# A gated recurrence and a bilinear feed-forward in one kernel: a new order of the first half, other engines for some of its work, and one transpose by DMA

## The chip, the cores and the metric

The kernel runs on one core of a Trainium2 chip. The core has TensorE (PE in the profile, PEld for its weight loads), VectorE (DVE), ScalarE (ACT), GpSimd (POOL) and SyncE (SP), which here only issues DMAs. The metric is the device time of one run in microseconds.

## The reference

Four sequences of 5824 tokens with 256 channels pass through a gated linear recurrence, and its output through a feed-forward without a nonlinearity:

```
log_a = 8 * sigmoid(r_gate) * log(clip(sigmoid(a_param)))
a     = exp(log_a);  norm = sqrt(max(1 - a*a, 1e-6))
h_t   = a_t * h_(t-1) + norm_t * sigmoid(i_gate_t) * x_t      # for every channel, along time
out   = (((h @ w1) * (h @ w2)) @ w3) @ w_out                  # 256 -> 1024 -> 1024 -> 256
```

## The kernel before

The 23296 tokens are cut into 47 chunks: two of 256 tokens that share tiles, 44 of 512, and one of 256. Time must lie along the free axis for the recurrence, so gates are turned from token rows to channel rows. For chunk c and channel half cb the steps are, with the one-letter names that the order uses:

- `r`, `i`, `x` load the three inputs; `R`, `I` are tanh on ScalarE (the sigmoid by way of tanh); `p` adds 1 to the input gate and `t` multiplies it by x, each half a chunk (`u_t`), on GpSimd or, if listed, on VectorE.
- `V` and `U` turn the decay gate and `u_t`. Chunks in `TURN_R` or `TURN_U` are turned by TensorE into PSUM (tile `ptr`), the others by a DMA transpose on SyncE into SBUF (tiles `rt` and `ut`).
- `d` is exp on ScalarE (`a_t`), `s` its square (`nrm`, on GpSimd, VectorE or ScalarE), `q` the root on ScalarE. tanh and exp share a table of ScalarE, the root has another: each change is an ACT_TABLE_LOAD.
- `g` multiplies the root by the turned `u_t` on VectorE, `h` is the scan on VectorE, `y` the cast of its result to bf16.
- `a` and `b` are the products with w1 and w2 (`pa`, `pb`), 128 features each for `a`, 256 for `b`; `c` copies `pa` to SBUF (`sa`, on ScalarE or, if in `DV_COPY`, on VectorE); `m` multiplies it by `pb` on VectorE (`g_t`).
- `D` multiplies `g_t` by the folded matrix w3 @ w_out (`po`), `e` copies the result out of PSUM, `o` stores it. The folding (`Ft`, `Fc`, `Fm`, `Fe`, tiles `ptw`, `w3t`, `pw`) is done in the kernel, between the first chunks, from eight pieces of w3 that are loaded (`L`) and cast (`C`). `W` is a pair of matmuls on the identity that has no use but to keep TensorE going while the first inputs arrive.

Nothing schedules this at build time. A string of 2449 words, ORDER, gives the order in which the steps are issued; since every engine works its own instructions in order, it fixes the order on each engine, DMA issues on SyncE included. Sets of indices (`DV_COPY`, `AC_SQUARE` and others) say which engine does a step. Buffers are rings: four PSUM slots (`po` in RINGS) are shared by `ptr`, `pa`, `ptw`, `pw` and `po`, two hold `pb`, and three each hold `sa` and `g_t`. A step that needs a slot waits until the last reader of its old content is done. The lines that matter here: `times` L175, `turn_pe` L194, `turn_dma` L207, `square` L225, `gated` L240, `scan` L254, `cast` L272, `copy` L325, `product` L332, `evac` L375, `fold_c` L432.

Of the kernel before, what the change touches and what calls it, by code (L numbers as in the profile page):

```python
# [664 lines left out]
```

## Time and profile before

| | |
|---|---|
| runs of the kernel before | 511.16, 511.36, 511.41 us (median 511.36) |
| span of the profiled execution, first to last instruction | 509.1 us |
| busy: TensorE, VectorE, ScalarE, GpSimd | 501.7, 431.8, 461.5, 318.0 us |
| ACT_TABLE_LOADs | 34 |

The span of the profiled execution is what the trace covers; its own launch time is not listed, and the runs are 2.3 us longer than its span. The busy time of TensorE is that of pipelined matmuls whose ends are modelled, so it is high even where matmuls start late. Times in the rows count from the start of the span.

### The profile page before, as it was taken

The page shows a single profiled execution, that of the slowest core. Times are in us where ns is not written, and L with a number is a line of the kernel's source. Part 1 is how long each engine was busy: PE and PEld are TensorE (multiplying, and loading weights), DVE is VectorE, ACT ScalarE, POOL GpSimd, SP SyncE. Part 2 cuts the span into 40 slices and gives each one's busy share as a digit, 9 for nine tenths or more (in the row PEclk, how much of TensorE's full clock was granted, in tenths as well). Part 3 has the DMA queues.
Part 4 walks back from the last instruction along what each step waited for, and adds up shares of the span by engine and source line. Part 5 has one row for each costly group of instructions (what it writes and reads, how often), then busy time and mean ns, then how long its engine had stood idle before and what let it go on. Part 6 is the DMA issues. An engine that isn't in the chain of part 4 may idle for free.

```text
span 509.1 us, 8891 instructions
## 1 busy us (share of the span) xinstructions
PE 501.7 (99%) x3225; PEld 308.3 (61%) x3225; DVE 431.8 (85%) x417; ACT 461.5 (91%) x708; POOL 318.0 (62%) x269
## 2 busy tenths in 40 slices
PE   7999999999999999999999999999999999999997
PEld 3767665665665656556656556565566655656566
DVE  6999999999999789879979799878877797959762
ACT  7999999998999999999999999998998979888543
POOL 1686677658658937964886973956647568580200
PEclk9999999999999999999999999999999999999999
DMA  8999999999989998896999997899886895252213
GB/s 317 410 411 345 335 316 282 305 286 259 310 220 298 279 285 247 211 302 196 247 305 327 254 286 148 252 243 227 210 246 164 235 298 161 85 166 62 65 51 104
DMA packets 178048, 124.06 MB, mean 244 GB/s; under 512 B 87378, under 2 KB 174036, under 8 KB 178004
## 3 DMA queue, kind: packets, MB, share of 16 engines
q1 hardware_dynamic: 178000, 123.50, 85.4%
q8 instruction: 25, 0.41, 0.4%
...
q10 hardware_dynamic: 4, 0.00, 0.0%
...
## 4 chain that ended last, share of the span: by engine, by line
PE 92%; ACT 3%; DMA 2%; POOL 1%; DVE 1%; issue 1%; SPq 1%; ACTq 0%; DVEq 0%
PE po L357 30%; PE pb L299 29%; PE pa L299 29%; DMA wf<-in_moe_w_dram 2%; PE pw L436 1%; ACT sa L322 1%; PE ptr L200 1%; PE ptw L425 1%; POOL u_t L192 0%; DVE h_t L270 0%; SPq L151 0%; ACT ot L322 0%; SPq L407 0%; ACT L168 0%; ACT L238 0%
## 5 line engine op out<-in xcount | busy, mean ns | idle before, releaser
L337 DVE TENSOR_TENSOR g_t<-sa,pb 128x1024 bf16<-128x1024 bf16 (+1 forms) x188 | 218.7, 1180 | 58.9 <-PE pb L299 27.6
L299 PEld LDWEIGHTS <-w_sb 128*128 128x128 bf16 x1504 | 146.4, 98 | 144.1 <-issue 1.4
L322 ACT CAST sa<-pa 128x512 bf16<-128x512 f32 (+1 forms) x332 | 179.8, 591 | 27.1 <-PE pa L299 18.9
L299 PE MATMUL pa<-y_t,w_sb 128*128 128x512 bf16 (+1 forms) x752 | 190.2, 372 | 0.2 <-ACT sa L322 0.2
L299 PE MATMUL pb<-y_t,w_sb 128*128 128x512 bf16 (+1 forms) x752 | 184.9, 372 | 0.2 <-ACT w_sb L414 0.2
L357 PE MATMUL po<-wp_sb,g_t 128*128 128x256 bf16 (+1 forms) x1464 | 177.6, 272 | 0.0
L357 PEld LDWEIGHTS <-g_t 128*128 128x128 bf16 x1464 | 142.5, 98 | 39.5 <-issue 0.3
L282 POOL CAST y_t<-h_t 128x1024 bf16<-128x1024 f32 (+2 forms) x47 | 53.8, 1145 | 140.2 <-DVE h_t L270 136.1
L192 POOL TENSOR_TENSOR u_t<-i_t,x_t 128x512 bf16<-128x512 f32 (+1 forms) x90 | 123.3, 1387 | 3.8 <-DMA ut<-u_t 1.8
L270 DVE TENSOR_TENSOR_SCAN h_t<-a_t,h_t,nrm 128x512 f32<-128x512 f32 (+1 forms) x92 | 121.1, 1343 | 1.6
L233 POOL TENSOR_TENSOR nrm<-a_t 128x512 f32<-128x512 f32 x70 | 78.4, 1137 | 7.0 <-ACT a_t L223 4.0
L223 ACT ACTIVATE a_t<-rt,la 128x512 f32<-128x512 bf16 (+1 forms) x82 | 66.1, 823 | 0.0
L322 ACT COPY ot<-po 128x512 f32<-128x512 f32 x84 | 49.1, 589 | 13.2 <-PE po L357 12.9
L173 POOL TENSOR_SCALAR i_t<-i_t 128x1024 f32<-128x1024 f32 (+1 forms) x45 | 55.4, 1233 | 8.3 <-ACT i_t L168 8.3
L251 DVE SCALAR_TENSOR_TENSOR nrm<-nrm,ut 128x1024 f32<-128x1024 f32 (+1 forms) x39 | 53.2, 1365 | 5.2 <-ACT nrm L238 5.2
L168 ACT ACTIVATE i_t<-i_t 128x1024 f32<-128x1024 f32 (+1 forms) x46 | 48.5, 1063 | 0.3 <-DMA i_t<-in_i_gate_dram 0.2
L238 ACT ACTIVATE nrm<-nrm 128x1024 f32<-128x1024 f32 (+1 forms) x47 | 48.4, 1040 | 0.2
L162 ACT ACTIVATE th_r<-r_t 128x1024 bf16<-128x1024 f32 (+1 forms) x41 | 43.5, 1064 | 0.0
L320 DVE CAST sa<-pa 128x512 bf16<-128x512 f32 x36 | 23.5, 684 | 1.4 <-PE pa L299 0.8
L238 ACT ACT_TABLE_LOAD x17 | 21.8, 1283 | 0.4
L287 PE MATMUL warm<-ident 128*128 128x512 bf16 x32 | 10.7, 473 | 1.6 <-DVE ident L441 1.6
L231 ACT ACTIVATE nrm<-a_t 128x512 f32<-128x512 f32 x18 | 11.4, 645 | 0.0
...
## 6 DMA issues: line engine op xcount, KB each, us to landing
r_t<-in_r_gate_dram SPq DMA_DIRECT2D x45, 512.0 KB, 5.2
i_t<-in_i_gate_dram SPq DMA_DIRECT2D x45, 512.0 KB, 6.0
x_t<-in_x_dram SPq DMA_DIRECT2D x45, 512.0 KB, 5.5
...
wf<-in_moe_w_dram SPq DMA_DIRECT2D x12, 512.0 KB, 10.5
wf<-in_moe_w_out_dram SPq DMA_DIRECT2D x2, 512.0 KB, 10.2
rt<-th_r SPq DMA_TRANSPOSE x41, 4.7
ut<-u_t SPq DMA_TRANSPOSE x39, 4.4
```

Of the source, the lines that this page charges most:

```text
L173: (nc.vector if c in DV_PLUS else nc.gpsimd).tensor_scalar(t, t, 1.0, 1.0, op0=ALU.add, op1=ALU.mult)
L192: (nc.vector if (c, half) in DV_HALF else nc.gpsimd).tensor_mul(out=u, in0=t, in1=xt)
L223: nc.scalar.activation(out=a, in_=pr, func=AF.Exp, scale=la4[:, cb:cb + 1], bias=la4[:, cb:cb + 1])
L233: (nc.vector if (c, cb) in DV_SQUARE else nc.gpsimd).tensor_mul(out=n, in0=a, in1=a)
L238: nc.scalar.activation(out=n, in_=n, func=AF.Sqrt, scale=-1.0, bias=1.0)
L251: nc.vector.scalar_tensor_tensor(out=n, in0=n, scalar=1e-3, in1=T["pu", c][:, :, cols], op0=ALU.max, op1=ALU.mult)
L270: nc.vector.tensor_tensor_scan(h[:, cb, :], a[:, cb, :], n[:, cb, :], init, ALU.mult, ALU.add)
L282: (nc.vector if key in DV_CAST else nc.gpsimd).tensor_copy(out=y, in_=h)
L299: nc.tensor.matmul(out=dst, lhsT=w_sb[:, cb, m * P:(m + 1) * P], rhs=T["y", gates_of(c)][:, cb, span(c, mp)], start=(cb == 0), stop=(cb == ...
L322: nc.scalar.copy(out=dst, in_=src_ps)
L337: nc.vector.tensor_mul(out=T["g", z][:, 2 * mp:2 * mp + 2, span(c, mp)], in0=T["sa", c, mp][:, :, :w], in1=T["pb", c, mp][:, :, :w])
L357: nc.tensor.matmul(out=po, lhsT=T["g", c][:, k, j * P:(j + 1) * P], rhs=wp_sb[:, k, cols], start=(k == 0), stop=(k == KD - 1), skip_group_ ...
```

## The change

Three things change. Chunk 6 leaves `TURN_U`: its `u_t` is turned by a DMA transpose. The sets that choose engines are new: `DV_COPY` grows from 36 to 62 entries and reaches to chunk 24, nine products `t` (`DV_HALF`) and a few other steps move to VectorE, `AC_SQUARE` grows from 18 to 23. And the first 1400 of the 2449 words of ORDER are in another order; from D23.2 on (the product of chunk 23's third block of 128 tokens) the words are the same. The number of table loads stays at 34.

```diff
-    TURN_U = {0, 2, 3, 4, 5, 6, 7}
+    TURN_U = {0, 2, 3, 4, 5, 7}
-    DV_HALF = set()
-    DV_SQUARE = {(0, 0), (0, 1), (5, 1), (9, 0)}
+    DV_HALF = {(2, 0), (12, 0), (15, 0), (18, 1), (19, 0), (21, 1), (23, 0), (25, 1), (26, 1)}
+    DV_SQUARE = {(0, 0), (0, 1), (26, 0)}
...
-    DV_CAST = {(1, 1)}
-    AC_CAST = {(1, 0)}
+    DV_CAST = {17, (1, 0)}
+    AC_CAST = {(0, 0), (0, 1)}
...
-    DV_EVAC = {(0, 0), (0, 1), (4, 1), (5, 1), (6, 1), (9, 0), (9, 1)}
-    FOLD_ACT = {('e', 0), ('e', 4), ('e', 5), ('e', 7)}
+    DV_EVAC = {(0, 1), (4, 0), (4, 1), (6, 1), (7, 0), (8, 1), (16, 0), (16, 1), (22, 1)}
+    FOLD_ACT = {('c', 3), ('c', 4), ('e', 1), ('e', 2), ('e', 3), ('e', 6)}
...
-    W_ACT = {('w2', 0), ('w3', 3)}
-    W_DVE = {('w1', 1)}
+    W_ACT = {('w3', 0)}
+    W_DVE = set()
...
-        r0 i0 x0 Lw1.1 Lw1.0 r2 i2 Lw2.0 Lw3.2 x2 E W13 A3. A0. A1. A2. R0.1 R0.0 W3 W10 V0.0 V0.1 I0 t0.1 d0.0 s0.0
+        E W9 W3 r0 A3. i0 A0. A1. W5 W7 W1 R0.0 V0.0 R0.1 V0.1 x0 Lw1.0 A2. I0 t0.0 W8 W6 t0.1 U0 d0.0 s0.0 W4
...
```

On ScalarE in the head, before (`nrm` is the root of chunk 0, `th_r` and `i_t` are chunk 2's gates, `y_t` is chunk 1's):

```order
L238 ACT_TABLE_LOAD
L238 ACTIVATE nrm<-nrm 128x2x256 x2
L160 ACT_TABLE_LOAD
L160 ACTIVATE th_r<-r_t 128x1024
L168 ACTIVATE i_t<-i_t 128x1024
L414 CAST w_sb<-wf 128x2x512
L280 CAST y_t<-h_t 128x256
L223 ACTIVATE a_t<-ptr,la_85 128x512 x2
```

and now (`y_t` is chunk 0's, both channel halves):

```order
L241 ACT_TABLE_LOAD
L241 ACTIVATE nrm<-nrm 128x2x256 x2
L163 ACT_TABLE_LOAD
L163 ACTIVATE th_r<-r_t 128x1024
L283 CAST y_t<-h_t 128x256 x2
L226 ACTIVATE a_t<-ptr,la_85 128x512 x2
L234 ACTIVATE nrm<-a_t 128x512
L171 ACTIVATE i_t<-i_t 128x1024
```

The cast of w2 and the tanh of chunk 2's input gate left this place; the two casts to chunk 0's `y_t` stand behind the table load and the tanh of `th_r`.

On VectorE at chunk 18, from the first scan of chunk 20 to the second (`g_t` is the product for chunk 18 or 19), before:

```order
L270 SCALAR_TENSOR_TENSOR h_t_2866<-a_t_2353,h_t_2790,nrm_2417 128x512
L337 TENSOR_TENSOR g_t_2899<-sa_2870,pb_2860 128x1024
L337 TENSOR_TENSOR g_t_2899<-sa_2826,pb_2909 128x1024
L337 TENSOR_TENSOR g_t_2899<-sa_2904,pb_2920 128x1024
L270 SCALAR_TENSOR_TENSOR h_t_2866<-a_t_2353,h_t_2790,nrm_2417 128x512
```

and now (`u_t` is chunk 21's):

```order
L273 SCALAR_TENSOR_TENSOR h_t_2858<-a_t_2296,h_t_2726,nrm_2463 128x512
L340 TENSOR_TENSOR g_t_2833<-sa_2781,pb_2862 128x1024
L340 TENSOR_TENSOR g_t_2833<-sa_2800,pb_2869 128x1024
L195 TENSOR_TENSOR u_t_2787<-i_t_2456,x_t_2713 128x2x2x128
L323 COPY ot_2909<-po_2892 128x512
L323 COPY ot_2930<-po_2913 128x512
L340 TENSOR_TENSOR g_t_2955<-sa_2843,pb_2940 128x1024
L340 TENSOR_TENSOR g_t_2955<-sa_2888,pb_2946 128x1024
L323 CAST sa_2975<-pa_2962 128x512
L273 SCALAR_TENSOR_TENSOR h_t_2858<-a_t_2296,h_t_2726,nrm_2463 128x512
```

Three products stood between the two scans; now four stand there, with one product `u_t`, two copies of `po` and one of `pa`.

On SyncE, where the decay gate of chunk 9 is turned (the first transpose into `rt`; the second is chunk 8's), before:

```order
L380 DMA out_dram<-ot 128x2x256
L151 DMA i_t<-in_i_gate_dram 128x4x256
L151 DMA r_t<-in_r_gate_dram 128x4x256
L211 DMA_TRANSPOSE rt<-th_r 128x8x128
L380 DMA out_dram<-ot 128x2x256
L151 DMA r_t<-in_r_gate_dram 128x4x256 x2
L211 DMA_TRANSPOSE rt<-th_r 128x8x128
```

and now (the transpose into `ut` is chunk 6's):

```order
L383 DMA out_dram<-ot 128x2x256
L154 DMA r_t<-in_r_gate_dram 128x4x256
L154 DMA x_t<-in_x_dram 128x1024
L214 DMA_TRANSPOSE ut<-u_t 128x8x128
L214 DMA_TRANSPOSE rt<-th_r 128x8x128
L383 DMA out_dram<-ot 128x2x256
L154 DMA i_t<-in_i_gate_dram 128x4x256
L383 DMA out_dram<-ot 128x2x256
L154 DMA i_t<-in_i_gate_dram 128x4x256
L214 DMA_TRANSPOSE rt<-th_r 128x8x128
```

The transpose into `ut` is new and stands ahead of the two others; TensorE's eight transposes of chunk 6 are gone.

## Rows read from the trace of the kernel before

**Rows 1.** Chain of waits by engine and line, 26.38 to 276.25 us (shares).
```profile
by line: PE pb L299 32.0%; PE pa L299 31.8%; PE po L357 31.5%; PE pw L436 2.4%; PE ptw L425 1.3%; PE ptr L200 1.1%
```

**Rows 2.** Pieces of that chain, 30 to 60 us: start, us, what.
```profile
35.25 0.45 PE ptr L200 x8
...
48.77 1.75 PE po L357 x16
...
50.52 1.73 PE pb L299 x8
```

**Rows 3.** TensorE by line and shape, 26.38 to 276.25: xcount | busy, mean ns | idle.
```profile
L299 PE MATMUL pa<-y_t,w_sb 128*128 128x512 bf16 x368 | 96.1, 379 | 0.0
...
L357 PE MATMUL po<-wp_sb,g_t 128*128 128x256 bf16 x720 | 88.4, 273 | 0.0
```

**Rows 4.** Busy us (instructions) of each engine by stretch, clock, DMA share, GB/s.
```profile
0.00:26.40 26.40, 22.32 (x162) 13.85 (x163) 20.64 (x45) 23.08 (x30) 11.41 (x18) 1.00 0.95 366
26.40:150.00 123.60, 123.60 (x841) 77.66 (x840) 121.38 (x134) 120.47 (x173) 85.06 (x70) 1.00 1.06 308
150.00:276.30 126.30, 126.30 (x779) 75.97 (x778) 108.36 (x89) 123.58 (x192) 90.48 (x72) 1.00 0.96 265
276.30:509.10 232.80, 229.49 (x1449) 140.80 (x1447) 181.41 (x152) 194.39 (x316) 131.07 (x111) 1.00 0.69 184
```

**Rows 5.** Pieces of the chain of waits, 0 to 26.38 us.
```profile
4.66 10.66 DMA wf<-in_moe_w_dram
...
17.52 2.51 POOL u_t L192 x2
...
20.07 0.51 PE ptr L200 x6
```

**Rows 6.** Timeline of the head: start, us, engine, line, operation, [idle before it].
```profile
7.08 0.69 DVE L189 SCALAR_TENSOR_TENSOR u_t<-i_t,x_t 128x512 bf16<-128x512 f32 x1 [1.62 <-DMA x_t<-in_x_dram]
...
9.31 1.15 ACT L238 ACTIVATE nrm<-nrm 128x512 f32<-128x512 f32 x2
...
10.36 0.75 DVE L248 SCALAR_TENSOR_TENSOR nrm<-nrm,ptr 128x256 f32<-128x256 f32 x2 [0.18 <-PE ptr L200]
...
10.48 1.28 ACT L160 ACT_TABLE_LOAD   x1
...
11.77 1.06 ACT L160 ACTIVATE th_r<-r_t 128x1024 bf16<-128x1024 f32 x1
...
13.11 1.04 PE L299 MATMUL pa<-y_t,w_sb 128*128 128x256 bf16 x8
...
22.73 2.49 DVE L270 TENSOR_TENSOR_SCAN h_t<-a_t,h_t,nrm 128x512 f32<-128x512 f32 x2
...
25.28 1.04 POOL L282 CAST y_t<-h_t 128x1024 bf16<-128x1024 f32 x1 [2.32 <-DVE h_t L270]
...
26.38 0.81 PE L299 MATMUL pa<-y_t,w_sb 128*128 128x512 bf16 x3
```

**Rows 7.** DMA transposes into ut, whole span: issue to landing.
```profile
DMA to landing us min/median/max: 2.7/4.4/6.9
```

**Rows 8.** Copies of pa on ScalarE and VectorE, whole span.
```profile
L322 ACT CAST sa<-pa 128x512 bf16<-128x512 f32 x324 | 177.1, 596 | 21.9 <-PE pa L299 14.9 <-DVE g_t L337 6.0
...
L320 DVE CAST sa<-pa 128x512 bf16<-128x512 f32 x36 | 23.5, 684 | 1.4 <-PE pa L299 0.8
```

**Rows 9.** VectorE's scans and gated products, 150 to 276.25 us: busy, mean ns | idle.
```profile
L270 DVE TENSOR_TENSOR_SCAN h_t<-a_t,h_t,nrm 128x512 f32<-128x512 f32 x25 | 35.4, 1434 | 0.5
...
L251 DVE SCALAR_TENSOR_TENSOR nrm<-nrm,ut 128x1024 f32<-128x1024 f32 x13 | 17.7, 1364 | 1.2 <-ACT nrm L238 1.2
```

**Rows 10.** Durations of scans and gated products, whole span: ns min/median/max, first to last start.
```profile
L270 DVE TENSOR_TENSOR_SCAN h_t<-a_t,h_t,nrm x92: 727/1279/2379, 13.2 to 487.8; 128x512 f32<-128x512 f32 x88, 128x256 f32<-128x256 f32 x4
...
L251 DVE SCALAR_TENSOR_TENSOR nrm<-nrm,ut x39: 686/1222/2105, 89.5 to 485.4; 128x1024 f32<-128x1024 f32 x38, 128x512 f32<-128x512 f32 x1
...
L251 DVE SCALAR_TENSOR_TENSOR nrm<-nrm,ptr x2: 1212/1216/1221, 61.0 to 65.9; 128x1024 f32<-128x1024 f32 x2
```

More of the change, by code (lines that the diff above doesn't have):

```diff
@@ new lines @@
+        c9.3.0 e8.1 i16 h11.0 o7.1 a10.3.0 c10.3.0 D8.1 D8.0 I16 a9.3.1 V16 a10.1.1 r17 e8.0 t12.0 a10.3.1
+        c9.3.1 V14 h11.1 y11 b9.3 m9.3 b10.3 a10.2.0 d16.0 U13 c10.1.1 c10.3.1 m10.3 a10.2.1 c10.2.1 x15 R17
+        a10.1.0 c10.1.0 b10.2 c10.2.0 d14.1 m10.2 p15 b10.1 d16.1 m10.1 s13.0 d14.0 p14 a11.0.0 s15.1 a11.0.1
+        c11.0.1 o8.1 c11.0.0 q12 a11.2.0 c11.2.0 b11.0 U12 t15.1 m11.0 a11.1.1 a11.3.1 c11.3.1 s16.0 o7.0
+        c11.1.1 g12 s14.0 D10.3 D10.2 e10.1 i17 t15.0 h12.0 a11.1.0 c11.1.0 h12.1 o8.0 D10.1 s16.1 a11.2.1
@@ new lines @@
+        d23.0 I24 s23.1 a18.2.0 V24 c18.2.0 D15.0 D15.1 e15.0 d24.1 o14.1 U20 r26 b18.0 m18.0 d24.0 a18.1.1
+        c18.1.1 a19.1.0 c19.1.0 I22 i25 o15.1 r27 a18.2.1 p22 t22.1 g20 h20.0 x23 b18.1 m18.1 c18.2.1 b18.2
+        m18.2 I23 V25 o15.0 t21.1 a19.0.1 x24 a19.0.0 c19.0.0 c19.0.1 I25 D16.2 D16.3 e16.1 U21 D16.1 D16.0
+        e16.0 o16.0 a19.3.0 a19.1.1 o16.1 b19.1 p25 b19.0 t22.0 c19.3.0 c19.1.1 m19.1 U22 R26 m19.0 a19.2.1
+        D17.3 p24 c19.2.1 d25.0 r32 h20.1 d25.1 s22.1 R27 a18.3.1 c18.3.1 D17.2 e17.1 a18.3.0 s21.0 c18.3.0
@@ new lines @@
+        R28 s25.1 c21.1.1 R30 c21.0.1 g23 b21.0 d27.0 a21.2.1 o18.0 D19.0 m21.0 D19.1 c21.2.1 e19.0 o19.0 I26
+        a21.1.0 c21.1.0 p26 h23.0 d27.1 s27.1 i27 a21.3.1 c21.3.1 a21.3.0 c21.3.0 x28 b21.1 a21.2.0 m21.1
+        c21.2.0 b21.3 m21.3 a22.1.0 c22.1.0 a22.1.1 c22.1.1 d26.1 s26.1 D19.3 b21.2 m21.2 R32 V28 a22.0.0
+        c22.0.0 t25.1 V30 t26.1 a22.2.0 c22.2.0 D19.2 e19.1 x27 a22.0.1 o19.1 I27 c22.0.1 b22.1 m22.1 b22.0
+        a22.2.1 c22.2.1 t25.0 h23.1 y23 D20.3 U25 a22.3.1 d28.1 s28.1 c22.3.1 D20.2 x29 e20.1 m22.0 b22.2
@@ new lines @@
+        m29.0 a29.2.1 e27.0 d33.1 a29.2.0 c28.3.0 c29.2.0 c29.2.1 x33 a28.3.1 c28.3.1 r38 g32 b29.1 m29.1 I36
+        b29.2 t31.1 t34.0 a30.0.0 m29.2 D27.2 c30.0.0 R35 s34.1 I35 o25.1 a30.0.1 b28.3 U31 d36.0 D27.3 e27.1
+        o27.0 m28.3 a29.3.0 s33.0 s33.1 p33 t34.1 b30.0 c30.0.1 c29.3.0 a30.2.0 a29.3.1 c29.3.1 i37 b29.3
+        a30.3.0 c30.2.0 d36.1 g31 m30.0 a30.1.0 V35 m29.3 b30.1 D28.0 D28.1 c30.3.0 o27.1 U34 x35 V37 a30.1.1
+        i38 q34 h31.0 h31.1 a30.2.1 h32.0 h32.1 b30.2 c30.1.0 e28.0 D28.2 D29.0 c30.1.1 t33.0 t33.1 o28.0
@@ new lines @@
+        m42.0 q43 g43 h43.0 h43.1 c42.1.0 c42.2.0 e41.0 U45 a42.1.1 a42.2.1 c42.1.1 q45 a42.3.0 c42.3.0 q44
+        D40.2 D40.3 e40.1 c42.2.1 b42.2 a42.3.1 o40.0 y43 c42.3.1 m42.1 x46 g45 m42.2 b43.0 U44 g44 o40.1
+        a43.0.1 a43.0.0 a43.1.0 c43.0.0 c43.0.1 b42.3 a43.1.1 a43.2.0 m42.3 m43.0 h44.0 h44.1 c43.1.0 c43.1.1
+        a43.3.0 c43.2.0 D41.2 D41.3 a43.2.1 b43.1 y44 c43.3.0 e41.1 m43.1 c43.2.1 o41.0 o41.1 a43.3.1 b43.2
+        D42.0 D42.1 e42.0 c43.3.1 o42.0 m43.2 h45.0 h45.1 b44.0 a44.0.0 a44.0.1 a44.1.1 a44.1.0 c44.0.0 y45
@@ L631 @@
+        b46.0 D44.2 D44.3 e44.0 b46.1 c46.0.1 c46.2.1 a46.1.1 D45.0 D45.1 c46.1.1 m46.0 e44.1 m46.1 b46.2
+        a46.3.1 a46.3.0 b46.3 D45.2 D45.3 e45.0 c46.3.0 c46.3.1 o44.0 o45.0 e45.1 o44.1 o45.1 m46.2 m46.3 D46.0
+        D46.1 e46.0 e46.1 o46.0 o46.1
         """
```

255 lines of the change are left out of this document (118 added, 137 removed), and 9 rows, old and new, of the table DV_COPY.

## The prediction

> **What bounds the kernel now.** I read the chain of waits first, then counts and busy time by stretch, and last the head instruction by instruction. From 26.38 us, where chunk 2's first product starts, to 276.25, where the new order falls back into the old one, every piece of the chain is TensorE's: the six shares of [rows 1] add up to 100.1%. A TensorE that is always on the chain may still stand still between matmuls, whose ends are modelled, so the reader should check by count. Matmuls follow each other at 1.73 / 8 = 0.216 us (512 columns) and 1.75 / 16 = 0.109 us (256 columns) [rows 2]. The stretch holds 368 of pa and as many of pb, 736 x 0.216 = 159.0; 720 of po, 720 x 0.109 = 78.5; and the 4.8% of the folding and the transposes, 12.0 [rows 1, 3]. That is 249.5 of 249.9 us: about 0.4 us is lost. ScalarE and VectorE only have to keep up there, and they do, at 97% and 98% up to 150 us, and at 98% and 86% from 150 to 276 [rows 4].
>
> What is not matmul work lies ahead of 26.38. There the chain runs over weight loads that land at 15.32, then over GpSimd to the two products for chunk 2's gated input, and to the transposes at 20.07 that wait for them [rows 5]. Beside it a chain on VectorE leads from chunk 0's input at 7.08 over the first gated product at 10.36 and chunk 2's scans, done at 25.22, to chunk 2's y at 26.32 [rows 6]. So there are three places: the head, 26 to 276 us, and the rest.
>
> **The change part by part.** The profiled span is 509.1 us and the median of the runs 511.36; the 2.3 us between them lie around the span, and I carry them over.
>
> *Chunk 6's gated input by DMA.* TensorE loses 8 transposes, 0.45 us [rows 2], all on the path: -0.45. SyncE gains one transpose, which lands 4.4 us after its issue at the median and 6.9 at worst [rows 7]. Its cover: it is issued once chunk 6's two products are there, and after them GpSimd still makes chunk 5's two (2.51 for two, [rows 5]), and VectorE a gated product (1.36, [rows 9]) and two scans (2.49, [rows 6]), before chunk 6's gated product is due: 6.4 us with nothing else between. It stays hidden; with 4.4 us of cover instead, VectorE would wait up to 2.5. Next behind it on SyncE is chunk 9's transpose, which ScalarE needs only after chunk 6's root, itself behind the same products and two squares.
>
> *The head.* All 32 warm matmuls remain, 30 of them now ahead of the first pa (26 before), in time that waits anyhow. On VectorE both halves of chunk 0's u now precede the two squares: four instructions from 7.08 end at about 9.6, a root of 0.6 follows on ScalarE, and the first gated product starts at about 10.25 instead of 10.36. But the casts to y for chunk 0 move from GpSimd to ScalarE, where a table load (1.28) and chunk 2's tanh (1.06) stand ahead of them, so the first pa starts at about 13.9 instead of 13.11 [rows 6]. On GpSimd w3's cast no longer stands ahead of chunk 2's sum. From 10.25 on VectorE carries the same work as before plus one half of chunk 2's u (0.65), and waits about half a us less for pb; I get chunk 2's scans done at 25.5 instead of 25.22. Chunk 2's first pa then waits for a PSUM slot that a copy frees at 26.7, with 0.45 us more folding behind it than before: 26.75 - 0.45 = 26.3 against 26.38, or -0.1. Each step of this walk is an estimate, good to some tenths. The ends: +0.8, if the late first pa passes on in full, and -1.9, if VectorE's chain is early enough that all of TensorE's standstills after 13.11 close (13.27 us up to 26.38, of which, by count, 10.1 are work and 1.3 warm matmuls). I take the walk's own -0.1.
>
> *Copies and products from ScalarE and GpSimd to VectorE.* Up to 276 us VectorE takes 26 more copies of pa, 2 more output copies, 9 products and a cast to y, and gives back 2 folding copies, a weight cast and one square. Of these 24 copies, 3 output copies, 7 products, a square and the cast belong to chunks 15 and later, after about 150 us. A copy of pa costs VectorE 23.5 / 36 = 0.65 us [rows 8], and so, by estimate, does each of the others except the cast, which I set at GpSimd's 1.04 [rows 6]: 35 x 0.65 + 1.04 = 23.8. VectorE was busy 108.4 of the 126.3 us there [rows 4]: 132.2 are asked of 126.3. Two things make room. Ahead of 150 us VectorE gives back about 1.2 us and has later work placed sooner. And the 108.4 contain standstills: in this stretch 25 scans take 1434 ns against 1279 at the median, 13 gated products 1364 against 1222, 25 x 0.155 + 13 x 0.142 = 5.7 us [rows 9, 10]; with fewer and otherwise placed GpSimd products part of that goes. 132.2 - 1.2 - 5.7 = 125.3, so VectorE would be full to the brim. A full VectorE need not cost anything: from 26.4 to 150 it was busy 121.4 of 123.6, and TensorE's chain was unbroken [rows 1, 4]. ScalarE sheds about 8 us there (27 copies at 177.1 / 324 = 0.55 [rows 8] against ten squares of about 0.65), and its 98% falls towards 92%: nothing by itself, since TensorE did not wait for it.
> The ends: -0.4 (all that was lost here goes) and +4.5 (all standstills stay: 132.2 - 1.2 - 126.3 = 4.7, less a little that scans a chunk ahead can absorb). The nearest row is the full stretch up to 150, where it cost nothing; a full VectorE under standstills as well is new, so I take the old 0.4 away and put 0.5 in its place: +0.1.
>
> The Trainium skill bears on those standstills. The row first: a gated product whose second input lies in PSUM (ptr) takes 1212 to 1221 ns, one that reads it from SBUF (ut) up to 2105 [rows 10]. The skill's page "SBUF — State Buffer", section "SBUF: two separate sides", says that a VectorE instruction with two SBUF inputs and a GpSimd instruction share one port pair as an exclusive lock, and whichever starts second fully waits. The trace agrees. By that rule the nine products and chunk 6's gated product become ten more instructions that can stand still; at 0.155 each that is 1.6 us more on VectorE, which speaks against moving products there, and would bring the overflow below nearer.
>
> *After 276 us.* The instructions and their order are the same, and VectorE has 51 us of idle time to catch up in [rows 4]: 0, within 0.3 either way.
>
> Sum: -0.45 - 0.1 + 0.1 + 0 = -0.45; span 508.6, time **510.9 us**.
>
> **The rivals.**
> *The head opens up.* If the walk is too slow in its landings, TensorE recovers 1.4 us of the 1.9 in the head, and the next stretch stays clean: -0.45 - 1.4 - 0.4 = -2.25, 509.1. For it: the first eight product pairs need only the first halves of w1 and w2, which are loaded earlier now. Against it: VectorE is without a break from 10 us on, in both orders.
> *VectorE overflows from 150 to 276 us* (the other side). Place: the products g_t of chunks 15 to 24, in one queue with the added copies; TensorE waits when the two pb buffers are not read in time. Price: up to 4.5; with two thirds of it, -0.55 + 3.0 gives 513.8. It decides once less than about 3 of the 5.7 us of standstills go. For it: 132 us of work for 126. Against it: the stretch up to 150.
> *Chunk 6's transpose lands late.* VectorE waits 2.5 us at a place where it is full: -0.55 + 2.5, about 513.3. Against it: the cover above.
>
> **How the numbers follow.** Forecast 0.44, head opens up 0.27, overflow 0.26, late transpose 0.03. No change and change are told apart at 0.2%, about 1.0 us. The forecast's own range is 510.2 to 512.0 and lies almost wholly within that; the head's case is faster, the other two are slower. With a little of the forecast's range given to faster, that is faster 0.29, within 0.43, slower 0.28. The range 509.3 to 513.9 leaves about one in ten out on each side.
>
> **What would show it.** Right: the chain from 26 to 276 us is TensorE's alone again; chunk 2's first pa starts between 26.0 and 27.2; VectorE is busy over 95% from 150 to 276 us, ScalarE under 95%; ptr has 88 matmuls. The overflow would show as VectorE in the chain there, or as pb's matmuls starting late behind g_t; standstills as scans far above 1279 ns. The forecast is wrong if chunk 2's pa starts more than 1 us away from 26.75, or if the stretch from there to the common order takes more than 251 us.

## The result and the profile after

The changed kernel takes 512.37 us (median of 10 runs, 511.62 to 514.66), the kernel before 511.38 in the same series (10 runs, 511.11 to 512.21). The ratio is 1.0025, with a 95% interval of 1.0013 to 1.0037: slower by about 1.0 us. The prediction was 510.9. Two of the changed kernel's ten runs have a mean granted clock of 0.997 and take about 2 us more; the other eight have a median of 512.3, so the difference does not rest on those two.

The two profiled spans are 510.5 and 509.1 us, 1.4 apart. In every later run that lists both, the time is 1.8 us above the span, so the profiled execution of before belongs to a run of about 510.9, 0.4 quicker than its median. Of the 1.4 about 1.0 is the change; where that execution gained its 0.4 the profiles don't show.

First the same stretches as [rows 4] in the kernel after (PE, PEld, DVE, ACT, POOL busy, then the granted clock, the DMA share and GB/s):

```profile
0.00:26.40 26.40, 20.93 (x155) 12.99 (x156) 20.54 (x42) 22.10 (x29) 12.30 (x17) 1.00 0.95 369
26.40:150.00 123.60, 122.91 (x828) 76.40 (x827) 121.03 (x134) 118.93 (x169) 84.83 (x72) 1.00 1.02 295
150.00:276.30 126.30, 126.30 (x782) 76.38 (x781) 123.99 (x122) 116.97 (x175) 69.54 (x57) 1.00 1.02 277
276.30:510.50 234.20, 231.02 (x1457) 141.54 (x1455) 182.72 (x156) 195.55 (x317) 133.05 (x111) 1.00 0.69 184
```

From 150 to 276 VectorE went from 108.4 to 124.0 us, ScalarE from 123.6 to 117.0, and TensorE stays full. What is lost lies in the first two rows. Counted as in the prediction (starts of matmuls against 0.216, 0.109 and 0.056 us), TensorE at chunk 2's first pa is 0.98 us further behind than before, it loses 1.4 us instead of 0.5 from there to the common order, and it has 8 transposes less, -0.45; together +1.5. Behind the common order nothing changed: that part takes 232.8 us in both.

The head, where [rows 6] and [rows 5] had the kernel before (timeline: start, length, engine, line, operation, idle time before it):

```profile
8.21 2.12 DVE L236 TENSOR_TENSOR nrm<-a_t 128x512 f32<-128x512 f32 x2
...
8.66 1.14 POOL L419 CAST w_sb<-wf 128x1024 bf16<-128x1024 f32 x1 [7.35 <-DMA wf<-in_moe_w_dram]
...
10.37 1.15 ACT L241 ACTIVATE nrm<-nrm 128x512 f32<-128x512 f32 x2 [0.91 <-DVE nrm L236]
11.03 0.75 DVE L251 SCALAR_TENSOR_TENSOR nrm<-nrm,ptr 128x256 f32<-128x256 f32 x2 [0.69 <-PE warm L290]
...
11.82 1.53 DVE L273 TENSOR_TENSOR_SCAN h_t<-a_t,nrm 128x256 f32<-128x256 f32 x2
...
14.40 0.63 PE L302 MATMUL pa<-y_t,w_sb 128*128 128x256 bf16 x4
...
14.84 0.77 POOL L285 CAST y_t<-h_t 128x256 bf16<-128x256 f32 x1 [2.62 <-DVE h_t L273]
...
15.56 1.09 POOL L419 CAST w_sb<-wf 128x1024 bf16<-128x1024 f32 x1
...
16.63 1.03 POOL L236 TENSOR_TENSOR nrm<-a_t 128x512 f32<-128x512 f32 x1
...
17.64 1.04 POOL L176 TENSOR_SCALAR i_t<-i_t 128x1024 f32<-128x1024 f32 x1
18.62 1.03 POOL L419 CAST w_t<-wf 128x1024 bf16<-128x1024 f32 x1
19.60 1.03 POOL L419 CAST w_sb<-wf 128x1024 bf16<-128x1024 f32 x1
20.46 0.72 DVE L195 TENSOR_TENSOR u_t<-i_t,x_t 128x512 bf16<-128x512 f32 x1
20.61 1.69 POOL L195 TENSOR_TENSOR u_t<-i_t,x_t 128x512 bf16<-128x512 f32 x1
...
22.91 1.28 DVE L251 SCALAR_TENSOR_TENSOR nrm<-nrm,ptr 128x512 f32<-128x512 f32 x2
24.11 2.45 DVE L273 TENSOR_TENSOR_SCAN h_t<-a_t,h_t,nrm 128x512 f32<-128x512 f32 x2
...
26.63 1.04 POOL L285 CAST y_t<-h_t 128x1024 bf16<-128x1024 f32 x1 [2.36 <-DVE h_t L273]
...
27.80 1.04 PE L302 MATMUL pa<-y_t,w_sb 128*128 128x512 bf16 x4
```

The squares in the kernel before:

```profile
7.69 1.29 DVE L233 TENSOR_TENSOR nrm<-a_t 128x512 f32<-128x512 f32 x2
```

Read four things. VectorE's two squares take 2.12 us beside GpSimd's cast of w1, where they took 1.29 before, so the root and the first gated product come 0.7 later. From 14.84 GpSimd works six tasks back to back ahead of its half of chunk 2's product, which ends at 22.30; in [rows 5] the two halves end at 20.03. VectorE has the other half (0.72 at 20.46), and its scans of chunk 2 end at 26.56 instead of 25.22. And the two queues meet: at 22.91, where chunk 2's gated product starts, TensorE's transposes of GpSimd's half (22.36 to 22.87) and the task ahead of it on VectorE (22.30 to 22.97) end within 0.1 us of each other. The profiler's chain goes over VectorE here; in e2 below, which has the same head, it goes over GpSimd from 14.63 to 22.11. So one execution can't say which of the two made the head late.

The one larger loss behind the head, in the same columns:

```profile
112.05 1.04 POOL L236 TENSOR_TENSOR nrm<-a_t 128x512 f32<-128x512 f32 x1 [3.51 <-ACT a_t L226]
112.05 2.12 DVE L273 TENSOR_TENSOR_SCAN h_t<-a_t,h_t,nrm 128x512 f32<-128x512 f32 x1
...
114.09 2.32 DVE L340 TENSOR_TENSOR g_t<-sa,pb 128x1024 bf16<-128x1024 bf16 x2
...
115.33 1.02 PE L302 MATMUL pb<-y_t,w_sb 128*128 128x512 bf16 x4 [0.59 <-DVE g_t L340]
```

A GpSimd square starts with chunk 10's second scan, which takes 2.12 instead of 1.28; the product behind it frees pb late, and TensorE loses 0.76 us.

### The profile page after: what moved, and what is told of

It reads as the page before. It is cut to its first block, busy times and chain, and to the rows that moved or that the text cites. A ratio compares the mean times of both kernels' runs of the same rounds, so it can differ in the third digit from the quotient of the medians.

```text
span 510.5 us, 8894 instructions
## 1 busy us (share of the span) xinstructions
PE 501.2 (98%) x3217; PEld 307.3 (60%) x3217; DVE 448.3 (88%) x451; ACT 453.6 (89%) x687; POOL 299.7 (59%) x256
## 4 chain that ended last, share of the span: by engine, by line
PE 74%; POOL 9%; issue 6%; DVE 6%; ACT 3%; DMA 2%; SPq 0%; POOLq 0%; DVEq 0%; ACTq 0%
PE po L360 25%; PE pb L302 24%; PE pa L302 24%; POOL u_t L195 3%; DVE g_t L340 2%; POOL i_t L176 2%; DVE h_t L273 2%; POOL nrm L236 2%; DMA ut<-u_t 1%; POOL y_t L285 1%; POOL w_t L419 1%; ACT sa L325 1%; DMA x_t<-in_x_dram 1%; DVE sa L323 1%; DVE nrm L251 1%
## 5 line engine op out<-in xcount | busy, mean ns | idle before, releaser
L325 ACT CAST sa<-pa 128x512 bf16<-128x512 f32 (+1 forms) x306 | 166.6, 587 | 34.5 <-PE pa L302 21.2
L285 POOL CAST y_t<-h_t 128x1024 bf16<-128x1024 f32 (+2 forms) x45 | 47.9, 1065 | 155.3 <-DVE h_t L273 152.9
L273 DVE TENSOR_TENSOR_SCAN h_t<-a_t,h_t,nrm 128x512 f32<-128x512 f32 (+1 forms) x92 | 117.9, 1312 | 1.8 <-DVE nrm L254 0.5
L195 POOL TENSOR_TENSOR u_t<-i_t,x_t 128x512 bf16<-128x512 f32 (+1 forms) x81 | 112.9, 1409 | 1.9 <-DMA ut<-u_t 0.7
L236 POOL TENSOR_TENSOR nrm<-a_t 128x512 f32<-128x512 f32 x66 | 75.4, 1158 | 18.4 <-ACT a_t L226 17.6
L226 ACT ACTIVATE a_t<-rt,la 128x512 f32<-128x512 bf16 (+1 forms) x82 | 65.9, 820 | 0.3 <-DMA rt<-th_r 0.2
L325 ACT COPY ot<-po 128x512 f32<-128x512 f32 x82 | 47.8, 586 | 13.1 <-PE po L360 12.2
L176 POOL TENSOR_SCALAR i_t<-i_t 128x1024 f32<-128x1024 f32 (+1 forms) x45 | 53.9, 1201 | 6.2 <-ACT i_t L171 6.1
L323 DVE CAST sa<-pa 128x512 bf16<-128x512 f32 x62 | 41.0, 682 | 0.9 <-PE pa L302 0.6
L234 ACT ACTIVATE nrm<-a_t 128x512 f32<-128x512 f32 x23 | 14.7, 638 | 0.2
```

The lines of the kernel that those rows point to most:

```text
L176: (nc.vector if c in DV_PLUS else nc.gpsimd).tensor_scalar(t, t, 1.0, 1.0, op0=ALU.add, op1=ALU.mult)
L195: (nc.vector if (c, half) in DV_HALF else nc.gpsimd).tensor_mul(out=u, in0=t, in1=xt)
L226: nc.scalar.activation(out=a, in_=pr, func=AF.Exp, scale=la4[:, cb:cb + 1], bias=la4[:, cb:cb + 1])
L236: (nc.vector if (c, cb) in DV_SQUARE else nc.gpsimd).tensor_mul(out=n, in0=a, in1=a)
L273: nc.vector.tensor_tensor_scan(h[:, cb, :], a[:, cb, :], n[:, cb, :], init, ALU.mult, ALU.add)
L285: (nc.vector if key in DV_CAST else nc.gpsimd).tensor_copy(out=y, in_=h)
```

## The experiments

*e1, e2, e3, e4* were timed against 511.28 of before (23 runs).

**e1: w1's first half loaded later.**

```diff
-x0 Lw1.0 A2. ... r2 W12
+x0 A2. ... r2 Lw1.0 W12
```

> The kernel after, with the load of w1's first half moved one place back on SyncE, behind chunk 2's r gate, so that GpSimd's cast of it starts after VectorE's two squares of chunk 0. Theory (the cast stands on the squares): the pair of squares takes 1.3 us instead of 2.12, the root starts at 9.6 to 9.8 instead of 10.37, the first gated product at about 10.3 instead of 11.03, chunk 2's first pa at 27.0 to 27.2 instead of 27.80, and the time falls by 0.6 to 0.8 us. Rival (the late y casts on ScalarE, behind the table load and the tanh, cost the time): squares shorter, but the first pa of chunk 0 still after 13.7 and chunk 2's first pa within 0.2 of 27.80; time unchanged within 0.2 us.

512.17 us. The squares took 1.29 and the first gated product started at 10.38, but chunk 2's first pa at 27.73. GpSimd's next cast (w2, at 11.60) now lay on the first scans, which took 2.10. The time fell by 0.2: the signs set for the rival. But that the edit moved the standstill isn't shown, for in the next run, e2, whose head has no edit, the two rows look the same:

```profile
8.24 1.29 DVE L236 TENSOR_TENSOR nrm<-a_t 128x512 f32<-128x512 f32 x2
...
11.01 2.13 DVE L273 TENSOR_TENSOR_SCAN h_t<-a_t,nrm 128x256 f32<-128x256 f32 x2
```

Its first gated product starts at 10.22 and its chunk 2's first pa at 27.60. One and the same order gives a long square in one execution and a long scan in another.

**e2: the square off the scan.**

```diff
-s13.1 h10.1 i13 y10
+h10.1 i13 y10 s13.1
```

> The kernel after, with GpSimd's second square of chunk 13 moved behind its cast of chunk 10's y, so that it no longer runs beside VectorE's second scan of chunk 10 (2.12 us at 112.05). Theory (the standstill of that scan makes TensorE wait 0.76 us at 114.5): the scan takes 1.1 to 1.3 us, TensorE loses under 0.15 us at that place, and the time falls by 0.6 to 0.8 us. Rival (VectorE is full and merely late there, so the wait moves on): the scan is shorter, but as much is lost within the next 10 us; time unchanged within 0.2 us.

512.06 us; span 510.1. Timeline of e2 at the same place:

```profile
111.85 1.28 DVE L273 TENSOR_TENSOR_SCAN h_t<-a_t,h_t,nrm 128x512 f32<-128x512 f32 x1
...
114.25 1.04 POOL L236 TENSOR_TENSOR nrm<-a_t 128x512 f32<-128x512 f32 x1
114.37 1.03 PE L302 MATMUL pb<-y_t,w_sb 128*128 128x512 bf16 x4
```

The scan is short and TensorE's 0.76 is gone; 0.17 and 0.27 came back at 130 and 140 us. The cause of that wait is shown; its whole price is not recovered.

**e3: chunk 6's input on TensorE again.**

```diff
-TURN_U = {0, 2, 3, 4, 5, 7}
+TURN_U = {0, 2, 3, 4, 5, 6, 7}
```

> The kernel after, with chunk 6's gated input turned on TensorE again (8 matmuls more), all else as it is. Theory (the 8 transposes are on the path): 0.4 to 0.5 us longer. Rival (the DMA's wait cost something that now goes): no longer, or shorter, than the kernel after.

512.91 us, 0.54 above the kernel after (0.46 when runs at clock 1.0 are compared): the 8 transposes are on the path. Its profile fell on a run of 515.99, and shows something else (windows; the granted clock is the third figure from the end):

```profile
12.00:16.00 4.00, 1.58 (x15) 0.95 (x14) 3.93 (x8) 3.87 (x6) 1.38 (x3) 0.98 1.04 416
16.00:19.00 3.00, 3.00 (x15) 2.11 (x14) 1.80 (x3) 2.98 (x5) 3.00 (x4) 0.50 1.04 402
```

The granted clock, 0.98, then 0.50 of full speed (1.2 of 2.4 GHz), fell after TensorE had been busy 1.58 of 4 us. In the kernel before, that stretch holds warm matmuls and products, 3.81 of 4 busy. The little work does not decide it by itself: the profile of the kernel after has 1.59 of 4 busy there and keeps 1.00. Ten of the 40 runs of this head (after, e1, e2, e3) have a mean clock of 0.997, with times 1.4 to 3.2 us above the others of their kernel; of before's 23 runs beside them none has (of 89 in all the series one).

**e4: the transpose by DMA alone, in the kernel before.**

```diff
-TURN_U = {0, 2, 3, 4, 5, 6, 7}
+TURN_U = {0, 2, 3, 4, 5, 7}
```

> The kernel before, with one thing of the change alone: chunk 6's gated input turned by DMA. Theory: TensorE's 8 transposes go and nothing else moves: 0.4 to 0.5 us shorter than the kernel before. Rival (the DMA is waited for in the old order, or gated products that read from SBUF stand still): within 0.2 us, or longer.

523.15 us, 12 us *longer*. Waits of e4 from 58 to 78 us:

```profile
DVE nrm L251 <- DMA ut<-u_t: 10.4, 1, 10.4
POOL u_t L192 <- DMA ut<-u_t: 9.2, 1, 9.2
```

Behind ten other transfers (e7, whose expectation speaks of seven, puts it ahead of them) SyncE issued it only at 68.10, 2.2 us after its gated product was due, and it landed 8.1 us later.

*e5 to e8* were timed against 511.32 of before (26 runs).

**e5: no weight cast beside the squares and first scans.** e1's move, and

```diff
-W_ACT = {('w3', 0)}
+W_ACT = {('w2', 0), ('w3', 0)}
```

> The kernel after, with w1's first half loaded behind chunk 2's r gate (as in the run before this one) and w2's first half cast by ScalarE, so that no GpSimd weight cast lies beside VectorE's squares or first scans of chunk 0. Theory (GpSimd's two casts hold up VectorE's queue, and moving one of them only moves the standstill): squares 1.3 us and first pair of scans 1.35 to 1.5, where the kernel after has 2.12 and 1.53 and the run with only w1 moved has 1.29 and 2.10; chunk 1's scans end at 14.5 to 14.8 instead of 15.42; chunk 2's first pa at 27.0 to 27.3 instead of 27.80; time 0.5 to 0.8 us shorter than the kernel after. Rival (the work added to VectorE and the three tasks put on GpSimd ahead of chunk 2's u set the end by themselves, whatever stands still before): chunk 2's first pa within 0.2 of 27.80.

512.66 us. Timeline of e5:

```profile
11.05 1.27 DVE L273 TENSOR_TENSOR_SCAN h_t<-a_t,nrm 128x256 f32<-128x256 f32 x2
...
17.57 1.05 POOL L176 TENSOR_SCALAR i_t<-i_t 128x1024 f32<-128x1024 f32 x1 [0.43 <-ACT i_t L171]
...
21.02 1.26 POOL L195 TENSOR_TENSOR u_t<-i_t,x_t 128x512 bf16<-128x512 f32 x1
...
22.89 1.28 DVE L251 SCALAR_TENSOR_TENSOR nrm<-nrm,ptr 128x512 f32<-128x512 f32 x2 [0.37 <-PE ptr L203]
```

Chunk 1's scans end 1.0 us earlier, at 14.39, and chunk 2's first pa starts at 27.78. My theory fell: GpSimd waited for ScalarE, which had the cast now, and brought chunk 2's input at the old time, so what VectorE had gained ended in a wait for it (0.37 at 22.89). None of its ten runs is at 0.997.

**e6: more warm matmuls in TensorE's wait.**

```diff
-WARM = [2] * 16
+WARM = [2, 2, 9] + [2] * 13
```

> The kernel after, with 7 warm matmuls more (1.5 us), put into TensorE's wait of 1.63 us for chunk 2's tanh, and nothing else. In the one profile that fell on such a run the granted clock was 0.5 of full speed from about 16 to 19 us, after TensorE had worked for only 0.6 us of the 4 us from 12 to 16, and 11 of 40 runs of kernels with this head, but none of 23 of the kernel before, show a mean clock of 0.997 and 2 us more. Theory (the empty stretch costs the clock): none, or at most one, of the runs shows 0.997, and the highest run is below 513.3; the other runs stay within 0.3 us of 512.2. Rival (these runs have another cause): about one run in four stays at 0.997 and above 513.4.

512.11 us (511.94 to 512.86); none of 11 runs at 0.997. (The expectation miscounts: ten runs of 40, and 1.6 us of work in the 4.) TensorE is busy 3.98 of the 4 us, and the clock stays at 1.00. At a rate of one in four, no such run in 11 has a chance of about 4%. Two later runs of kernels built on e6 (one of five of e9, one of five of e11) show 0.997 again. This profile is also the closest to the prediction's walk on VectorE: squares of 1.29, the first gated product at 10.08, chunk 1's scans done at 14.21. Yet chunk 2's gated product starts at 22.48 and its scans end at 26.14: with VectorE early, GpSimd's product still makes them late.

**e7: e4 with the transpose issued earlier.** e4's edit, and

```diff
-V9 ... x10 a4.0.0 U6 D3.0
+U6 V9 ... x10 a4.0.0 D3.0
```

> The kernel before, with chunk 6's gated input turned by DMA as the only change of work, but issued ahead of chunk 9's r-gate transpose instead of behind seven more transfers. Theory (it is SyncE's queue that made the DMA 10 us late in the order before): issue at about 61.6 us, VectorE's wait for it under 1 us, time 0.3 to 0.5 us shorter than the kernel before (510.8 to 511.0). Rival (a transposed input from SBUF costs VectorE standstills or a wait in this order wherever it is issued): 0 to 3 us longer than the kernel before.

513.27 us. VectorE no longer waits for the DMA. At 65.9 us, first before, then e7:

```profile
65.86 1.21 DVE L251 SCALAR_TENSOR_TENSOR nrm<-nrm,ptr 128x1024 f32<-128x1024 f32 x1
65.89 1.28 POOL L192 TENSOR_TENSOR u_t<-i_t,x_t 128x512 bf16<-128x512 f32 x1
```

```profile
65.96 1.22 DVE L251 SCALAR_TENSOR_TENSOR nrm<-nrm,ut 128x1024 f32<-128x1024 f32 x1
66.00 2.31 POOL L192 TENSOR_TENSOR u_t<-i_t,x_t 128x512 bf16<-128x512 f32 x1
```

With its second input in PSUM (ptr) the gated product left GpSimd alone; with both in SBUF (ut) GpSimd's product, started 0.04 later, took 1.03 more. The third of them then fell on a scan (2.21), and TensorE waited 1.2 for it. It waited once more, 0.7 at 68.70, for ScalarE's copy of an output block; e17 shows why.

**e8: chunk 2's product on GpSimd alone.**

```diff
-DV_HALF = {(2, 0), (12, 0), ...
+DV_HALF = {(12, 0), ...
```

> The kernel after, with both halves of chunk 2's gated-input product on GpSimd (one is on VectorE), all else as it is. Theory (VectorE's queue and GpSimd's both reach chunk 2's gated product at the same time, 22.9): VectorE gives up 0.65 us, but GpSimd's second product ends at 23.1 to 23.5, so that chunk 2's first pa starts 0.2 to 0.6 us later and the time is 0.2 to 0.6 us longer. Rival (VectorE's queue alone sets the end): chunk 2's first pa 0.4 to 0.6 us earlier, time 0.4 to 0.6 us shorter.

512.33 us, the same as after; neither expectation came. That GpSimd pays what VectorE is spared would explain it and is not shown: the profile fell on a run at clock 0.997, with the two products done at 22.92 and chunk 2's first pa at 28.87.

*e9 to e11* were timed against 511.19 of before (9 runs), *e12 to e14* against 511.36 (10 runs).

**e9: chunk 2's input ahead of the weight casts** (on e6).

```diff
-i2 Lw3.2 ... m0.1 Cw3.2 ... Lw2.1 Cw2.1 x2 t2.0 ... t2.1 ... a0.2.0 Ft2 Fc2 ... b0.2 m0.2 V3 U2 ... g2 h2.0 h2.1
+i2 x2 Lw3.2 ... m0.1 t2.0 t2.1 ... Lw2.1 Cw2.1 Cw3.2 ... a0.2.0 U2 a0.2.1 c0.2.0 g2 b0.2 m0.2 Ft2 V3 ... h2.0 h2.1 Fc2
```

> The kernel of the run with more warm matmuls (512.11), with chunk 2's gated input put ahead of two weight casts: its x is loaded before w3's and w2's halves, GpSimd makes its half product before it casts them, VectorE its half one product earlier, TensorE turns it before chunk 0's last-but-one pair's gate product, and the fold of w3's piece comes after it. Theory (the head ends late because GpSimd works seven tasks back to back, 14.84 to 22.30, before chunk 2's input is ready): the last transposes of it start by 21.3 instead of 22.36, chunk 2's first pa at 26.5 to 27.3 instead of 27.8, time 511.1 to 511.8. Rival (VectorE's queue behind the first gated product sets the end, 0.65 more work in it than before): chunk 2's first pa at 27.5 or later, time 511.9 to 512.3.

514.74 us. The last transposes start at 21.16, but chunk 2's scans end only at 26.27: VectorE's half product took 1.50 beside GpSimd's. Chunk 2's first pa starts at 30.27, because I had put the copy Fc2 so late that TensorE stood still behind it:

```profile
26.91 1.05 PE L439 MATMUL pw<-wo_sb,w3t 128*128 128x256 bf16 x8 [1.93 <-DVE w3t L323]
```

**e10: eight more copies on VectorE** (on e6):

```diff
-DV_COPY = {(0, 0, 0), ...
+DV_COPY = {(17, 2, 0), (18, 3, 0), (20, 0, 0), (20, 2, 0), (21, 1, 0), (22, 0, 0),
+    (23, 3, 0), (24, 3, 0), (0, 0, 0), ...
```

> The kernel of the run with more warm matmuls (512.11), with 8 more copies of pa of chunks 17 to 24 on VectorE, taken from ScalarE. VectorE was busy 124.0 of the 126.3 us from 150 to 276; 8 x 0.65 = 5.2 us more make 129.2 of 126.3. Theory of the prediction's rival (VectorE overflows there, TensorE waits for pb): 1 to 3 us longer, with waits of pb's matmuls behind g_t between 170 and 276 us. Theory of the prediction (a full VectorE costs nothing, standstills give way or scans absorb it): within 0.3 us of 512.1, TensorE loses under 0.5 us between 150 and 276.

517.87 us, 5.8 more than e6 for 5.2 us of copies. VectorE is busy 123.1 of 126.3 us (124.0 in e6). TensorE's waits lie from 228 to 262 us behind VectorE's copies of pa, and not, as expected, behind pb. Window and timeline of e10:

```profile
150.00:276.30 126.30, 122.77 (x739) 73.41 (x753) 123.13 (x125) 110.34 (x163) 68.62 (x56) 1.00 0.97 266
```

```profile
228.78 2.78 PE L360 MATMUL po<-wp_sb,g_t 128*128 128x256 bf16 x24 [0.77 <-DVE sa L323]
```

**e11: e9 with e2's move.**

```diff
-s13.1 h10.1 i13 y10
+h10.1 i13 y10 s13.1
```

> Both repairs in one kernel: chunk 2's gated input ahead of the weight casts with more warm matmuls, and chunk 13's second square behind chunk 10's y. If the two losses stand apart, their gains add: 0.3 to 0.4 us below the run with the first alone, 510.8 to 511.5, and so level with the kernel before or up to 0.5 us under it. If the square's wait only moves on, as half of it did when it was moved alone, no more than 0.2 below.

514.57 us, 0.17 below e9: no more than the wait moving on.

**e12: both queues relieved.** e5's edits and e9's (VectorE's half of chunk 2's product one copy later), 4 warm matmuls more, and

```diff
-b1.3 r4 Lw3.0 Lw3.1 Cw3.1 R4 Fm2 Fe2 ... b1.2
+b1.3 r4 Lw3.0 Lw3.1 Cw3.1 R4 ... b1.2 Fm2 Fe2
```

> The kernel after with both queues of the head relieved at once: w1's first half loaded behind chunk 2's r gate and w2's first half cast by ScalarE (so that VectorE's first part has no standstill), and chunk 2's input ahead of the two weight casts on GpSimd, its transposes and gated product earlier; the fold of w3's first piece (which held TensorE up for 2 us in the run before) now behind the first products of chunk 1's third pair; 4 warm matmuls more. Theory (two queues pin the head together, so that relieving either gains nothing): chunk 2's input is turned by 21.0, VectorE's scans of chunk 2 end at 25.3 to 25.8 instead of 26.57, chunk 2's first pa starts at 26.3 to 27.0 and the time is 511.0 to 511.7. Rival (something third, such as pb's two slots or ScalarE, pins it too): chunk 2's first pa at 27.4 or later, time 511.9 to 512.5 or above.

514.44 us. Chunk 2's input is turned by 20.9 and the gated product starts at 21.12, 1.8 earlier than in the kernel after; yet the scans end at 26.42. They took 3.19 beside GpSimd's casts of w_out, and four of five runs have a clock of 0.996 or 0.997:

```profile
20.00:21.00 1.00, 0.49 (x8) 0.45 (x8) 0.52 (x1) 0.79 (x1) 1.00 (x2) 1.00 1.10 399
21.00:22.00 1.00, 0.81 (x6) 0.39 (x4) 0.88 (x2) 0.65 (x2) 1.00 (x2) 0.52 1.08 420
```

Chunk 2's first pa starts at 30.20, the sign set for something third. One such thing is ScalarE's tanh, for which TensorE waits:

```profile
27.33 0.62 PE L203 MATMUL ptr<-ident,th_r 128*128 128x128 bf16 x8 [0.90 <-ACT th_r L163]
```

The lower clock explains little of the time: the fifth run, at 1.0, took 514.03, 0.4 less than the median.

**e13: e12 with e2's move** (the diff of e2).

> The same with chunk 13's second square behind chunk 10's y. If the gains add, 0.3 to 0.4 us below e12 (510.7 to 511.4); if the wait only moves on, within 0.2 of it.

514.31 us, within 0.2 of e12. So no repair of the new head succeeded, and whether the two queues alone pin it isn't settled.

**e14: eight copies fewer on VectorE** (on e6), out of DV_COPY:

```diff
-(17, 0, 0), (18, 1, 0), (19, 2, 0), (21, 3, 0), (22, 1, 1), (23, 1, 0), (24, 0, 1), (24, 2, 0)
```

> The kernel of the run with more warm matmuls (512.11), with 8 of VectorE's copies of chunks 17 to 24 given back to ScalarE, which was busy 117.0 of 126.3 us there: VectorE 124.0 - 5.2 = 118.8, ScalarE about 121.5. Theory (the full VectorE costs nothing as the kernel stands, only the next copies do): within 0.3 us of 512.1. Rival (it costs already): 0.4 us or more shorter.

513.68 us, 1.6 longer than e6, which neither expectation had, although VectorE and ScalarE then had 118.9 and 118.8 of 126.3 us to do. TensorE waited for a copy of pa that stood on ScalarE behind a table load, a root and an output copy:

```profile
200.60 1.06 ACT L241 ACTIVATE nrm<-nrm 128x1024 f32<-128x1024 f32 x1
...
203.68 1.58 PE L360 MATMUL po<-wp_sb,g_t 128*128 128x256 bf16 x13 [0.73 <-ACT sa L325]
```

Whether the full VectorE costs something by itself can't be read from it. It also bears on e10: where a copy stands in its queue can cost as much as how many there are, so the 5.8 of e10 is not shown to be the price of fullness alone.

*e15 to e17* were timed against 511.43 of before (21 runs).

**e15: one edit of the new head in the kernel before.**

```diff
-DV_HALF = set()
+DV_HALF = {(2, 0)}
```

> The kernel before with one edit of the change in the head: one half of chunk 2's gated-input product on VectorE instead of GpSimd (0.65 us more on VectorE there, 1.25 less on GpSimd). If VectorE's queue sets the end of the head before, as the prediction's walk had it: scans of chunk 2 done at 25.5 to 25.9 instead of 25.22, time 0.2 to 0.6 us longer. If GpSimd's product does, as the chain of waits has it: chunk 2's input is turned up to 1.2 us earlier and the time is 0.2 to 0.8 us shorter. If both reach chunk 2's gated product together: within 0.2 us.

512.08 us, +0.65, ratio 1.0014 (1.0005 to 1.0022). The half took 1.18 on VectorE, beside a GpSimd cast, and the scans end at 26.32 instead of 25.22:

```profile
19.19 1.18 DVE L192 TENSOR_TENSOR u_t<-i_t,x_t 128x512 bf16<-128x512 f32 x1
...
23.87 2.45 DVE L270 TENSOR_TENSOR_SCAN h_t<-a_t,h_t,nrm 128x512 f32<-128x512 f32 x2
```

**e16: the other edit.**

```diff
-p2 t2.0 t2.1 U2 c1.0.0 m1.1 Cw2.1
+p2 Cw2.1 t2.0 t2.1 U2 c1.0.0 m1.1
```

> The kernel before with the other edit alone: GpSimd casts w2's second half ahead of chunk 2's gated-input products instead of behind them (1.03 us). Theory (the weight casts ahead of the products make the new head late): transposes of chunk 2's input done at 21.6 instead of 20.58, its scans at 25.7 to 26.2 instead of 25.22, time 0.4 to 1.0 us longer. Rival (there is a spare microsecond at that place): within 0.2 us.

512.28 us, +0.85, ratio 1.0018 (1.0009 to 1.0027); the scans end at 26.80. GpSimd in e16:

```profile
18.38 1.04 POOL L416 CAST w_sb<-wf 128x1024 bf16<-128x1024 f32 x1 [0.53 <-DMA wf<-in_moe_w_dram]
19.38 2.50 POOL L192 TENSOR_TENSOR u_t<-i_t,x_t 128x512 bf16<-128x512 f32 x2
```

Each edit alone makes the old kernel slower by more than half of what the whole change does. How late each makes the head is less sure. e15's first loads land as before's do (chunk 0's x at 7.08), so its 1.10 is the edit's; in e16 loads land 0.2 to 0.4 us later and the cast waits 0.53 for one, so up to 0.4 of its 1.58 may be the landing.

**e17: e7 with three buffers for u_t.**

```diff
-"u": 2, "rt": 2, "ut": 6
+"u": 3, "rt": 2, "ut": 5
```

> The kernel before with chunk 6's gated input turned by DMA, issued ahead of chunk 9's r-gate transpose (as in e7), and three buffers instead of two for the products u_t (for which the turned inputs have five instead of six). Theory (GpSimd's third product had to wait until the DMA had read its buffer, 5.70 instead of 3.74 us for three, and TensorE 1.2 us for that product): the three take 3.8 us again, no wait of TensorE from 60 to 80 us, time 0.3 to 0.6 us shorter than the kernel before, 510.7 to 511.0. Rival (the DMA in this order costs in another way): 0.5 us or more longer than before.

513.70 us. The three products take 5.70 as in e7, so the buffer was not the reason for that; the standstill is, and TensorE again waits 1.1 us for a product. The rest is another wait, the same as in e7. SyncE works in order, and chunk 6's transpose waits there for its products with other transfers behind it: in e7 chunk 9's transpose goes out at 62.35 instead of 56.38 before, an output store at 63.70 instead of 59.61. ScalarE's next copy of an output block waits until that store has read its buffer, and TensorE waits for the copy. Waits of e17 from 58 to 80 us:

```profile
ACT ot L322 <- DMA out_dram<-ot: 1.2, 1, 1.2
PE pa L299 <- ACT ot L322: 0.8, 1, 0.8
```

So chunk 6's early transpose costs twice: 1.1 to 1.2 us by the standstill and 0.7 to 0.8 by the late store, near the 1.95 us by which e7 is longer than before. This run's head has no edit, and yet its chunk 2's scans end at 26.53, where before, e4 and e7 have 25.01 to 25.22: the head itself varies by over a microsecond from one execution to another. Here chunk 0's x lands at 7.93 instead of 7.08, and w3's cast comes 1.3 later.

No version ran under the kernel before.

## Why the prediction was wrong, step by step

**The sum's base.** I carried 2.3 us over as lying around the span. It is 1.8; the rest was that the profiled execution was a quick one. The forecast took 0.45 from the median, so it stays 510.9 either way, and this is not what failed.

**Chunk 6's transposes: right.** -0.45 by count, and 0.46 in e3 at the same clock; g6 did not wait. That it stays hidden was right for this order only: of the same edit in the old order the runs made +12 us (issued late) and +2 us (issued early, but with its gated product on GpSimd's product and a store held up behind it). The prediction priced the gated product that reads SBUF at 0.155 us of VectorE, beside its sum; the price that counted in e7 was 1.03 on GpSimd and 0.94 on the scan that it then met, and 0.7 by the store.

**The head: the step that failed**, -0.1 predicted, +0.98 by the profiles. (The size varies with the execution. Before, e4 and e7, with the old head, have chunk 2's first pa at 26.38, 26.38 and 26.48; the kernel after, e2 and e6, with the new one, e6 with more warm matmuls, at 27.80, 27.60 and 27.37; but e17, with the old head and late loads, at 27.69.) The walk left out two things. First, "the first gated product starts at about 10.25" was 11.03: the walk had no standstill of the squares under GpSimd's cast, although the next paragraph spoke of such standstills from 150 us on. Second, it followed VectorE and SyncE and never added up GpSimd, which [rows 5] show on the path: a cast to y, two more weight casts and a square, 3.9 us together, came to stand ahead of chunk 2's product there. "I get chunk 2's scans done at 25.5" was 26.56.

Taking away one of the two did not bring the head back. In the kernel after, both queues reach chunk 2's gated product at 22.9. In e6 VectorE starts as the walk had it, and the scans still end at 26.14, 0.6 behind the walk; in e5 the standstill is gone too, and VectorE waits for GpSimd's product instead. On the other side, e9 and e12 bring GpSimd's product earlier, and the scans end at 26.27 and 26.42. And the half given to VectorE was no free relief. e15 and e16 show what two of the edits cost the old kernel by themselves, +0.65 and +0.85 us; that such edits sum up to the new head is argued, since no repair brought it back. TensorE itself is nearly tied there: in the kernel after it also waits 1.6 us for ScalarE's tanh and 0.8 for VectorE's cast to y, and its chunk 2's pa follows other matmuls without a gap, with y ready 0.1 us earlier.

The criterion that I had set (chunk 2's pa more than 1 us from 26.75) was met: 27.80. The other (more than 251 us from there to the common order) was not: 249.9. The late first pa (13.9 predicted, 14.40 measured) goes with one thing more: TensorE was busy only 1.6 of 4 us around it, and the clock fell behind that place in a profile of such a run (e3); ten of 40 runs of this head show 0.997. That the stretch is the cause is likely by e6 and not shown: e5 has none in ten runs with 2.54 of 4 busy, and e8 three in eleven with 2.02.

**26 to 276 us: the mechanism right, a term missing.** VectorE ran full (98%) and ScalarE at 93% as forecast, TensorE was full from 150 on, and the overflow didn't come. The standstills that had to give way did, by these rows of the kernel after against [rows 9]:

```profile
L273 DVE TENSOR_TENSOR_SCAN h_t<-a_t,h_t,nrm 128x512 f32<-128x512 f32 x25 | 32.3, 1320 | 0.4
L254 DVE SCALAR_TENSOR_TENSOR nrm<-nrm,ut 128x1024 f32<-128x1024 f32 x13 | 16.2, 1247 | 0.0
```

25 x 0.041 + 13 x 0.025 = 1.4 us are left of 5.7, against the rival's threshold of 3 that go. "Full to the brim" fits e10, whose next 5.2 us cost 5.8, though e14 leaves open how much of that is the place of the copies. What the +0.1 lacked is a single standstill ahead of 150, 0.76 us at 114.5 (e2), in the stretch that I had taken as proof that a full VectorE costs nothing.

**After 276 us: 0, right.** Of the rivals, *the head opens up* had the wrong sign, *overflow* and *late transpose* did not happen, though e4 shows a late transpose one edit from the kernel before, and e10 something like the overflow one edit from e6. The case that did, a head late on the queues of GpSimd and VectorE, had no chance of its own. The size, +0.98, lies near the upper end of the head's term, +0.8, which was given for another reason, the late first pa.

The Trainium skill, page "SBUF — State Buffer", section "SBUF: two separate sides", says that of a GpSimd instruction that reads SBUF and a VectorE instruction with two SBUF inputs the one that starts second waits for the whole of the other. The traces of the kernel after and of e7 agree nearly in full: the squares took 0.83 us more beside a cast of 1.14 (8.66 us), the scan 0.84 more beside a square of 1.04 (112.05 us), and GpSimd's product in e7 1.03 more beside a gated product of 1.22 (66.00 us). Twice VectorE is the one that waits, in e7 GpSimd.
